# The store in SBUF, and the places that loads write into, moved to multiples of 256 bytes

## The chip, the cores and the metric

The kernel runs on one core of a Trainium2 chip. The core has five engines: TensorE (PE in the profile, with its weight loads as PEld), VectorE (DVE), ScalarE (ACT), GpSimd (POOL) and SyncE (SP), and it moves data with 16 DMA engines. Its on-chip memory SBUF has 128 partitions. The metric is the device time of one execution in microseconds (us): 740.67 us before the change, the median of three runs that lay between 740.43 and 740.8 us.

## The reference

Two layers of attention, each followed by a gated MLP, run one after the other on one token for a batch of 4, with the same weights both times. All data are float32.

```python
def _A_ref(x, k_cache, v_cache, wq, wo):           # x: 4 x 1 x 640
    q = (x @ wq)                                   # 640 x 4096: 32 heads of 128
    k, v = k_cache[:, :, -1024:], v_cache[:, :, -1024:]   # 4 x 32 x 1024 x 128 each
    p = softmax(q . k * 128 ** -0.5)
    return (p . v) @ wo                            # 4096 x 640
def _B_ref(x, W_gate, W_up, W_down):               # 640 x 1728, 640 x 1728, 1728 x 640
    gate, up = x @ W_gate, x @ W_up
    return (gate * (gate > 0) * up) @ W_down

x = x + _A_ref(layernorm(x), ...)
x = x + _B_ref(layernorm(x), ...)
x = x + _A_ref(layernorm(x), ...)
x = x + _B_ref(layernorm(x), ...)
```

The keys and values of the last 1024 positions, together 134 MB, are read once per layer, and so are the weights, except for what is kept on chip between the layers.

## The kernel before

The host lays all inputs that have to be loaded out as three wide arrays of 128 rows, one row to a partition. `heads` holds the query weights (q), keys (k), values (v) and output weights (o) of 27 heads in the order in which they are used, 255,744 floats to a row. `kept` holds the same for the last 5 heads, 47,360 floats to a row. `mlp` holds the weights of the MLP, 25,920 floats to a row. `heads` and `mlp` are loaded in both layers. `kept` is loaded once and stays in SBUF until the second layer's attention has used it.

Nearly all of SBUF is one tile, `store`, of `STORE` floats in each partition. The function `load` (L156) treats it as a ring: it takes the next piece of the list `todo`, finds the place `at` where it goes, cuts the piece where it would run over the end of the store or of a quarter of it (`QUARTERS`, for large pieces), and stops when a float of that place is still in use (`live`). Otherwise it issues one DMA on SyncE's queue (L185), which copies a range of columns of all 128 rows. `kept` has places of its own, at its own offsets, and where the ring starts anew is set by a few numbers: `FIRST` for the first layer's first pieces, `FIRST_MLP` for the first piece of the first layer's `mlp`, `FRONT` for what lies behind the kept heads. Each time a matmul's operand has been used, `done` frees its floats and calls `load` again. All this is done while the program is built. In the program there are 107 loads on one queue, each with the waits that its place needs. The first 1024 columns go to a tile of their own, `first_q` (L160).

A load copies one contiguous run of bytes into each partition, so a load of 13,312 columns is 128 rows of 53,248 bytes. The trace has one packet for each row, eight to a DMA engine, and one packet of 4 bytes per load and DMA engine. 64 of the 107 loads have rows of 8 KB and more, 30 of them rows of 52 to 55 KB (about 13,300 columns). The other 43 have shorter rows, down to 256 columns. They stand mainly in and around the first layer's MLP, where the ring has little room, because `kept` fills most of the store.

TensorE computes queries (L316, L321), scores (L345), transposes of the probabilities (L358), values (L373) and output projections (L403) group by group of up to four heads, and the MLP by L457, L492 and L501. It reads every operand straight out of the store. VectorE and ScalarE do the softmax and small copies.

Where the tiles lie follows from their sizes, in the order in which the pools allot them. The small tiles end at byte 9,440 of each partition, which is 36 x 256 + 224. So `store` begins 224 bytes behind a multiple of 256. Column c of the store has the address 9,440 + 4c. The ring mostly starts at column 0 or at multiples of 64 columns, so that nearly all loads begin 224 bytes behind a multiple of 256. The exceptions: the first four loads into the store, which start from `FIRST`, begin at 160; one load of the first `mlp` piece, at `FIRST_MLP`, begins at 128; `first_q` and one load of the second layer (rows of 53,376 bytes, at column 40,416) begin at 96. In HBM all rows begin on multiples of 256 bytes, except for that last load and one of 1,920-byte rows, which begin 128 behind.

Of the kernel before, what the change touches and what calls it, by code (L numbers as in the profile page):

```python
# [7 lines left out]
F32 = mybir.dt.float32  # L8
# [5 lines left out]
P = 128  # L14
# [43 lines left out]


HELD = 1024  # L60
STORE = 54944 - HELD
QUARTERS = [STORE // 4, STORE // 2, STORE // 4 * 3, STORE]
FRONT = KEPT * 2 * (D + KV)
FIRST, FIRST_MLP = 10928, 53160


def size_of(what, i):
# [23 lines left out]
def decode_kernel(ctx: ExitStack, tc: tile.TileContext, x, source, sel, out):  # L91
# [7 lines left out]
    ps_y = ctx.enter_context(tc.tile_pool(name="ps_y", bufs=1, space=bass.MemoryType.PSUM))  # L99
    ps_m = ctx.enter_context(tc.tile_pool(name="ps_m", bufs=2, space=bass.MemoryType.PSUM))  # L100
    big = ctx.enter_context(tc.tile_pool(name="big", bufs=1))
    store = big.tile([P, STORE], F32, name="store")
    first_q = big.tile([P, HELD], F32, name="first_q")
    ctx.enter_context(tc.manual_schedule())
# [45 lines left out]

    live = [False] * STORE
    at, spare = FIRST, True
# [3 lines left out]
    def load(part=False):  # L156
# [4 lines left out]
        while todo:  # L161
# [4 lines left out]

            ends = QUARTERS if end - lo > 16384 else [STORE]
            room = min(e - to for e in ends if e - to >= 2048 or e == STORE)
            hi = max(c for c in cuts if c <= min(end, lo + room))
# [413 lines left out]
```

## Time and profile before

| what | value |
|---|---|
| median of 3 runs | 740.67 us (740.43 to 740.8) |
| span of the profiled execution, first to last instruction | 738.5 us |
| the runs' median less that span | 2.2 us |
| PE busy | 453.3 us (61%) |
| DVE busy | 75.1 us (10%) |
| ACT busy | 47.1 us (6%) |
| packets of SyncE's load queue | 15,552, 312.24 MB |

The trace gives the span of the profiled execution; the only times of whole executions are those of the runs. The profile lists DMA queues with their packets, megabytes, and the time that their packets took as a share of what 16 DMA engines have in the stretch looked at. Such a row can be asked for any window of the span. It counts packets that begin in the window, and their whole time, so that a share can be a little over or under 100% in a short window; the share times 16 times the window's length, divided by the number of packets, is the mean time of one packet. SyncE's load queue is q1. The rows q8 and q14 are loads of instructions, and q10 is ScalarE's queue.

### The profile page before, as it was taken

The page shows a single profiled execution, that of the slowest core. Times are in us where ns is not written, and L with a number is a line of the kernel's source. Part 1 is how long each engine was busy: PE and PEld are TensorE (multiplying, and loading weights), DVE is VectorE, ACT ScalarE, POOL GpSimd, SP SyncE. Part 2 cuts the span into 40 slices and gives each one's busy share as a digit, 9 for nine tenths or more (in the row PEclk, how much of TensorE's full clock was granted, in tenths as well). Part 3 has the DMA queues.
Part 4 walks back from the last instruction along what each step waited for, and adds up shares of the span by engine and source line. Part 5 has one row for each costly group of instructions (what it writes and reads, how often), then busy time and mean ns, then how long its engine had stood idle before and what let it go on. Part 6 is the DMA issues. An engine that isn't in the chain of part 4 may idle for free.

```text
span 738.5 us, 8243 instructions
## 1 busy us (share of the span) xinstructions
PE 453.3 (61%) x3749; PEld 143.2 (19%) x3749; DVE 75.1 (10%) x279; ACT 47.1 (6%) x88; POOL 0.2 (0%) x4
## 2 busy tenths in 40 slices
PE   1657366556567636726689898445756545656685
PEld 0111111011122201202333232101211111122242
DVE  1011000010001001101101211001010100001010
ACT  1100000000000000000101110000000000000110
POOL 0000000000000000000000000000000000000000
PEclk9889787867689867969999999867778977668899
DMA  9999999999999999999999999999999999999996
GB/s 393 448 409 439 441 425 428 447 417 431 441 431 424 426 446 411 445 418 420 410 397 394 427 430 427 443 427 446 425 431 423 447 426 425 438 434 427 422 423 281
DMA packets 15738, 312.85 MB, mean 424 GB/s; under 512 B 1748, under 2 KB 2260, under 8 KB 7512
## 3 DMA queue, kind: packets, MB, share of 16 engines
q1 hardware_dynamic: 15552, 312.24, 99.0%
q8 instruction: 29, 0.48, 0.3%
q10 hardware_dynamic: 152, 0.09, 0.0%
q14 instruction: 5, 0.04, 0.0%
HBM read 312.24 MB, written 0.08 MB: 423 GB/s over the span
## 4 chain that ended last, share of the span: by engine, by line
DMA 52%; PE 32%; another core or an unknown queue 14%; issue 1%; DVE 1%; ACT 0%; SPq 0%; DVEq 0%; ACTq 0%
DMA store<-in_heads 30%; PE ps L345 13%; DMA store<-in_mlp 12%; PE po L373 10%; DMA store<-in_kept 10%; PE qp L316 2%; PE pp L358 1%; PE y L403 1%; PE qp L321 1%; PE gu L457 1%; PE qt L333 1%; PE ot L393 0%; PE po L258 0%; PE so L384 0%
## 5 line engine op out<-in xcount | busy, mean ns | idle before, releaser
L345 PE MATMUL ps<-store,qT 128*4 128x512 f32 x1024 | 161.3, 700 | 106.2 <-DMA store<-in_heads 101.1
L373 PE MATMUL po<-store,pT 128*16 128x512 f32 x1024 | 155.9, 720 | 108.0 <-DMA store<-in_heads 97.4
L373 PEld LDWEIGHTS po<-store,pT 128*16 128x16 f32 x1024 | 34.7, 110 | 214.1 <-issue 131.0
L345 PEld LDWEIGHTS ps<-store,qT 128*4 128x4 f32 x1024 | 29.3, 93 | 220.1 <-DMA store<-in_heads 116.1
L349 DVE TENSOR_REDUCE nm<-ps 128x1 f32<-128x1024 f32 x18 | 22.0, 1225 | 243.4 <-PE ps L345 243.4
L353 ACT ACTIVATE probs<-ps,nm 128x1024 f32<-128x1024 f32 x18 | 20.0, 1113 | 353.3 <-DVE nm L349 345.6
L316 PE MATMUL qp<-store,xT 128*32 128x512 f32 (+2 forms) x136 | 23.6, 623 | 24.6 <-DMA store<-in_heads 24.5
L403 PE MATMUL y<-store,oT 128*4 128x160 f32 x512 | 26.0, 332 | 8.8 <-DMA store<-in_heads 7.6
L369 DVE COPY pT<-pp 128x16 f32<-128x16 f32 x128 | 17.1, 168 | 135.6 <-PE po L373 135.6
L457 PE MATMUL gu<-store,xT 128*32 128x256 f32 (+1 forms) x300 | 23.9, 379 | 9.1 <-DMA store<-in_mlp 8.6
L380 ACT COPY gates<-po 128x512 f32<-128x512 f32 x16 | 9.4, 586 | 244.3 <-PE po L373 244.3
L358 PE MATMUL pp<-sel_sb,probs 128*128 128x128 f32 x144 | 20.5, 289 | 0.0
L358 PEld LDWEIGHTS pp<-sel_sb,probs 128*128 128x128 f32 x144 | 18.1, 151 | 0.0
L321 PE MATMUL qp<-store,xT 128*32 128x512 f32 (+4 forms) x48 | 17.5, 512 | 0.0
L326 DVE TENSOR_SCALAR gates<-qp,rstd 128x512 f32<-128x512 f32 (+2 forms) x18 | 12.4, 690 | 49.9 <-PE qp L321 44.5
L386 DVE RECIPROCAL r<-so 128x16 f32<-128x16 f32 x18 | 4.6, 257 | 122.6 <-PE so L384 122.6
L403 PEld LDWEIGHTS y<-store,oT 128*4 128x4 f32 x512 | 13.3, 93 | 19.4 <-DMA store<-in_heads 8.2
L457 PEld LDWEIGHTS gu<-store,xT 128*32 128x32 f32 x300 | 11.0, 115 | 18.1 <-DMA store<-in_mlp 7.4
L492 PE MATMUL y<-store,hT 128*4 128x160 f32 x208 | 11.3, 329 | 3.4 <-DMA store<-in_mlp 3.2
L333 PE MATMUL qt<-sel_sb,gates 128*128 128x128 f32 x64 | 12.3, 316 | 0.0
L393 PE MATMUL ot<-sel_sb,gates 128*128 128x128 f32 x72 | 11.4, 279 | 1.2 <-DVE gates L377 1.2
L333 PEld LDWEIGHTS qt<-sel_sb,gates 128*128 128x128 f32 x64 | 7.6, 155 | 18.6 <-issue 17.3
(62 smaller groups left out, 108.5 us busy)
## 6 DMA issues: line engine op xcount, KB each, us to landing
store<-in_heads SPq DMA_DIRECT2D x18, 6656.0 KB, 54.2
store<-in_heads SPq DMA_DIRECT2D x7, 6912.0 KB, 52.2
store<-in_heads SPq DMA_DIRECT2D x2, 6592.0 KB, 54.6
store<-in_heads SPq DMA_DIRECT2D x2, 5376.0 KB, 65.5
store<-in_mlp SPq DMA_DIRECT2D x16, 640.0 KB, 6.9
store<-in_kept SPq DMA_DIRECT2D x4, 2048.0 KB, 40.4
store<-in_heads SPq DMA_DIRECT2D x3, 2560.0 KB, 20.9
store<-in_heads SPq DMA_DIRECT2D x1, 6896.0 KB, 46.1
```

Source lines behind the costliest of these rows:

```text
L316: nc.tensor.matmul(qp[g][32 * c:32 * c + 32, :], xT[:, B * c:B * c + 32], part(layer, "q", g, c * n, n), start=True, stop=c > 0 and not sp ...
L321: nc.tensor.matmul(qp[g][32 * a:32 * a + 32, a * m:a * m + m], xT[:, B * c:B * c + 32], part(layer, "q", g, c * n + a * m, m), start=False ...
L326: nc.vector.tensor_scalar(gates[:, :len(HEADS[g]) * P], qp.pop(g), rstd, SCALE, op0=ALU.mult, op1=ALU.mult)
L333: nc.tensor.transpose(qt[:, i], gates[:, i * P:(i + 1) * P], ident)
L345: nc.tensor.matmul(ps[32 * b:32 * b + SIDE, j, :], qT[:, at:at + SIDE], part(layer, "k", h, lo, 512), start=i == 0, stop=i == n - 1, tile_ ...
L349: nc.vector.tensor_reduce(nm[g], ps.rearrange("p j n -> p (j n)"), axis=AX.X, op=ALU.max, negate=True)
L353: nc.scalar.activation(probs, ps.rearrange("p j n -> p (j n)"), AF.Exp, bias=nm.pop(g), accum_out=sums[g])
L358: nc.tensor.transpose(pps[g][c // 4][:, c % 4, :], probs[:, c * P:(c + 1) * P], ident)
L369: nc.vector.tensor_copy(to[:, 4 * j:4 * j + 4], pp[j][:, :, i:P:32])
L373: nc.tensor.matmul(po[32 * a:32 * a + SIDE * B, :], t[:, at:at + SIDE * B], part(layer, "v", h, c * 512, 512), start=i == 0 and c < 4, sto ...
L403: nc.tensor.matmul(y[32 * a:32 * a + B], o[:, i], part(layer, "o", h, a * QUARTER, QUARTER), start=False, stop=last and h == HEADS[g][-1], ...
L457: nc.tensor.matmul(gus[j][32 * g:32 * g + 32, :2 * n], xT[:, B * c:B * c + 32], get(layer, "mlp", lo, 2 * n), start=c == 0, stop=c == KC - ...
```

## The change

The constants become multiples of 64 floats, and a tile of 8 floats (32 bytes) that nothing uses is allotted ahead of the store:

```diff
 HELD = 1024
-STORE = 54944 - HELD
+STORE = 53888
 QUARTERS = [STORE // 4, STORE // 2, STORE // 4 * 3, STORE]
 FRONT = KEPT * 2 * (D + KV)
-FIRST, FIRST_MLP = 10928, 53160
+FIRST, FIRST_MLP = 10944, 53248
...
     big = ctx.enter_context(tc.tile_pool(name="big", bufs=1))
+    big.tile([P, 8], F32, name="pad")
     store = big.tile([P, STORE], F32, name="store")
```

The store now begins at byte 9,472 = 37 x 256 and has 53,888 floats instead of 53,920. `first_q` follows it at 225,024 = 879 x 256. All loads but one begin on a multiple of 256 bytes in SBUF. The exception is the load of 53,376-byte rows, which begins 128 behind one (its rows in HBM begin 128 behind one too). The lines of the kernel below the new tile have numbers higher by one.

The instructions of TensorE, VectorE, ScalarE and GpSimd are the same, in the same order. On SyncE's queue two pairs of neighbouring loads are cut elsewhere, because the end of the store has moved by 32 floats. The first pair is the last `heads` piece of the first layer, where it runs over the end of the store (the names are the tile written and the array read, then partitions x columns). On SP, before:

```order
L185 DMA store<-in_heads 128x2560
L185 DMA store<-in_heads 128x13728
L185 DMA store<-in_heads 128x480
L185 DMA store<-in_kept 128x8192
L185 DMA store<-in_kept 128x4096 x4
```

and now:

```order
L186 DMA store<-in_heads 128x2560
L186 DMA store<-in_heads 128x13568
L186 DMA store<-in_heads 128x640
L186 DMA store<-in_kept 128x8192
L186 DMA store<-in_kept 128x4096 x4
```

160 columns have moved from the first load to the second.

The second pair is in the first layer's MLP, where the ring comes to the end of the store for the first time. On SP, before:

```order
L185 DMA store<-in_mlp 128x512
L185 DMA store<-in_mlp 128x768
L185 DMA store<-in_mlp 128x1280 x3
L185 DMA store<-in_mlp 128x512
L185 DMA store<-in_mlp 128x768 x2
L185 DMA store<-in_mlp 128x512
```

and now:

```order
L186 DMA store<-in_mlp 128x512
L186 DMA store<-in_mlp 128x768
L186 DMA store<-in_mlp 128x1280 x3
L186 DMA store<-in_mlp 128x768
L186 DMA store<-in_mlp 128x512
L186 DMA store<-in_mlp 128x768
L186 DMA store<-in_mlp 128x512
```

The load of 512 columns and the first of 768 behind the three of 1280 have changed places, and so 256 columns have moved from the second to the first. In both kernels the second of the pair waits for TensorE to have used the load at `FIRST_MLP`.

## The prediction

> **What bounds the kernel now.** I read the page's DMA part first, then the windows by stage, then the chain.
>
> ```profile
> span 738.5 us, 8243 instructions
> ...
> DMA  9999999999999999999999999999999999999996
> ...
> DMA packets 15738, 312.85 MB, mean 424 GB/s; under 512 B 1748, under 2 KB 2260, under 8 KB 7512
> ...
> q1 hardware_dynamic: 15552, 312.24, 99.0%
> q8 instruction: 29, 0.48, 0.3%
> q10 hardware_dynamic: 152, 0.09, 0.0%
> q14 instruction: 5, 0.04, 0.0%
> ...
> DMA 52%; PE 32%; another core or an unknown queue 14%; issue 1%; DVE 1%; ACT 0%; SPq 0%; DVEq 0%; ACTq 0%
> ```
>
> The 16 DMA engines are busy in every slice but the last, and the load queue q1 alone takes 99.0% of their time. The windows by stage (first layer's attention, its MLP, two parts of the second attention, second MLP; busy time of each engine, granted clock, DMA share, GB/s) say the same:
>
> ```profile
> 2.00:361.00 359.00, 202.32 (x1507) 57.39 (x1511) 33.80 (x124) 22.05 (x36) 0.00 (x0) 0.81 1.00 430
> 361.00:402.00 41.00, 34.40 (x432) 14.27 (x428) 4.55 (x19) 4.28 (x14) 0.00 (x0) 1.00 1.01 397
> 402.00:464.00 62.00, 55.51 (x472) 17.73 (x464) 12.44 (x39) 6.95 (x12) 0.00 (x0) 0.94 1.01 425
> 464.00:712.00 248.00, 143.48 (x1072) 43.53 (x1071) 20.86 (x83) 12.11 (x22) 0.00 (x0) 0.79 1.00 432
> 712.00:738.50 26.50, 17.57 (x283) 10.27 (x283) 2.43 (x10) 1.67 (x5) 0.00 (x0) 0.87 0.78 324
> ```
>
> The DMA share is 1.00 up to 712 us, while PE, the next engine, is busy for about three fifths of the time. The chain ends on a load as well, followed by one set of matmuls and a copy:
>
> ```profile
> 712.18 22.84 DMA store<-in_mlp
> ...
> 735.07 0.50 PE y L492 x8
> ...
> 735.59 0.32 DVE probs L523
> ```
>
> So a nanosecond saved on a packet should reach the end, times the packets that one DMA engine has in sequence. There are 107 loads of 8 rows for each engine, 856 rows (with the output's store, 108 x (128 + 16) gives the row's 15,552). Of all packets 15,738 - 7,512 = 8,226 have 8 KB or more; less the 34 of q8 and q14 these are 8,192, or 512 long rows to an engine, and 344 are short.
>
> **What a row costs now.** A row's time is its bytes at some rate, and something besides. Two rows of the DMA view part them, one of mostly long rows (window 70 to 240 us) and one of shorter ones (418 to 462 us):
>
> ```profile
> q1 hardware_dynamic: 1536, 73.30, 99.9%
> ...
> q1 hardware_dynamic: 1100, 18.77, 100.3%
> ```
>
> The first is 0.999 x 16 x 170 = 2717.3 us of packet time, the second 1.003 x 16 x 44 = 706.1 us. Scaled to the first one's megabytes (x 3.905) the second has 4,296 packets and 2757.4 us: 2,760 more packets take 40.1 us more, 14.5 ns each. What is left of the first is 27.2 bytes per ns and DMA engine. At most 14.5 x 856 = 12.4 us of the kernel, then, is beside the bytes.
>
> Next, windows that hold rows of one length and one start alone, in this order: 14.7 to 21.4 us (55,296 bytes, starting 160 behind a multiple of 256), 39.6 to 53.7 (53,248 at 160), 71.5 to 84.5 (53,248 at 224), 103 to 117.3 (55,296 at 224), 310.1 to 322.3 (54,912 at 224), 563 to 576.3 (55,168 at 224) and 579.3 to 589.6 (53,376 at 96):
>
> ```profile
> q1 hardware_dynamic: 50, 2.76, 95.2%
> ...
> q1 hardware_dynamic: 112, 5.96, 97.8%
> ...
> q1 hardware_dynamic: 110, 5.86, 104.2%
> ...
> q1 hardware_dynamic: 112, 6.19, 100.2%
> ...
> q1 hardware_dynamic: 96, 5.27, 100.1%
> ...
> q1 hardware_dynamic: 100, 5.52, 96.1%
> ...
> q1 hardware_dynamic: 82, 4.38, 98.1%
> ```
>
> Share x 16 x length / packets gives means of 2041.1, 1970.0, 1970.3, 2046.9, 2035.4, 2045.0 and 1971.6 ns. Less the bytes at 27.2 per ns, the extra is 8.2, 12.3, 12.7, 14.0, 16.6, 16.8 and 9.2 ns. The first window, before the DMA engines have been held up, stands apart. The other six go by one count: how many 256-byte blocks of SBUF a row touches, each at 256 / 27.2 = 9.41 ns whether it is filled or not. These are 209, 209, 217, 216, 217 and 209 blocks. The measured means lie 2.9, 3.2, 4.5, 2.5, 2.6 and 4.5 ns above, a spread of 2.0 instead of 7.6. A row of whole blocks that starts at 160 or 224 touches one block more than it fills; the 54,912- and 55,168-byte rows waste one and a half, and the 53,376-byte row only half of one. I take this as the reason why rows cost 13 ns beside their bytes and not 8.
>
> **The change part by part.** *Starts on multiples of 256 bytes.* A row of whole blocks then wastes none. What remains is the cost of a packet that nothing holds up. The lower end is the block count alone: the 9.4 ns of one block are saved on each of 856 rows, 8.1 us. The other end is the 9.2 ns of the 53,376-byte row, the best in the steady stretches: 4.0 ns saved. Between them I take the 8.2 ns of the first window, since it has the same odd start and still runs below its block count (217 x 9.41 = 2042.4 ns), so it shows another limit, of the packet itself.
>
> Long rows: the mean of 12.7 and 14.0, the two common lengths, is 13.3, and 13.3 - 8.2 is 5.1 ns. Of 512 rows 16 are in the first two loads, of which I take it that they cost 8.2 already; 496 x 5.1 = 2.5 us. Short rows: two windows of 5,120-byte rows, 368.3 to 368.8 and 382.6 to 383.1 us, read
>
> ```profile
> q1 hardware_dynamic: 42, 0.22, 105.0%
> ...
> q1 hardware_dynamic: 40, 0.20, 99.0%
> ```
>
> or 200.0 and 198.0 ns against 188.2 for the bytes: 11.8 and 9.8, mean 10.8, so 2.6 ns x 344 = 0.9 us. With 9.2 in place of 8.2 it is 4.1 x 496 + 1.6 x 344 = 2.6 us.
>
> Here a rule stands against a row. The Trainium skill, "DMA: Bandwidth & Descriptors", section "How a descriptor splits into AXI transactions", says that a first transaction begins at the 256-byte boundary below the start, and that the unused bytes still cost beats of 32 bytes. By it a start at 224 costs 7 beats, one at 160 costs 5, and alignment saves an estimated 7.0 us. The trace does not agree on the step between them, 12.7 against 12.3 ns where the rule has 2.4 ns, and no run here shows a start at 0.
>
> *The part that does not reach the end.* In the first layer's MLP the chain runs for a while on TensorE, from
>
> ```profile
> 381.24 0.62 PE gu L457 x2
> ...
> 390.58 0.40 PE y L492 x6
> ...
> 390.99 6.05 DMA store<-in_mlp
> ```
>
> 9.7 us, in which earlier data are worth nothing. About seven loads land in it; 7 x 8 x 2.6 ns is 0.15 us. I take off 0.3 us, since later loads there wait for places that TensorE frees.
>
> *The two pairs that are cut elsewhere.* Bytes and count stay. The first pair lies under a queue that is 43 us deep (its 480-column piece, 240 KB, from issue to landing):
>
> ```profile
> store<-in_heads SPq DMA_DIRECT2D x1, 240.0 KB, 42.8
> ```
>
> so where it is cut costs nothing while that queue is there, and without it the 160 columns that change sides, 8 x 640 bytes / 27.2 = 0.2 us. In the second pair the first load grows by 256 columns and lands 8 x 1,024 / 27.2 = 0.3 us later; the second ends where it did. At 0 to 0.3 us I take 0, since TensorE needs the second right after. The unused tile issues nothing. That TensorE's operands start elsewhere I price at nothing: PE is hidden under the DMA share of 1.00 above, and no row shows a price by start.
>
> Sum: 2.5 + 0.9 - 0.3 = 3.1 us off the span of 738.5, or 735.4. What lies around the span, 2.2 us up to the median of 740.67, is not touched. That gives **737.6 us**, 0.4% less. With 9.2 ns a row it is 738.4, and the rounding of the shares, 1 ns a row or 0.9 us, widens the two to 736.7 and 739.3.
>
> **The rivals.** *The whole block is saved.* If the 8.2 ns of the first window are themselves due to the odd start, all 856 rows gain up to 9.4 ns, and the time is 740.7 - 8.1 = 732.6 us. For it speaks that the block count fits six windows to 2 ns; against it, that the first window does not follow it. The rule named above would give nearly this, an estimated 733.7 us.
>
> *No change.* The hold-up may be on the HBM side, or in handing out packets, and only look like a count of blocks, since just three kinds of waste occur. That 160 and 224 cost the same speaks for it. Then it stays at 740.7, give or take 0.5. Against it: the 53,376-byte rows are longer than the 53,248-byte ones by 4.7 ns worth of bytes and take only 1.3 ns more.
>
> *Slower: the engines in step.* The uneven hold-ups keep the 16 DMA engines apart. When they start together, on the first load (2.4 to 3.2 us, 4,096-byte rows),
>
> ```profile
> q1 hardware_dynamic: 58, 0.24, 88.4%
> ```
>
> a row takes 195.1 ns for 150.6 ns of bytes, 36 ns over the 8.2. If freed engines fell into step and a fifth of the rows paid that, it were 0.2 x 856 x 36 = 6.2 us, less the 3.1 gained: 743.8 us. It decides from about 10% of the rows on (3.1 / (856 x 0.036)). Against it: ten microseconds after that start the first window above shows only 8.2.
>
> **How the numbers follow.** My forecast gets 0.52: the block count is well borne out, the floor is a choice. The whole block gets 0.18, no change 0.20, slower 0.10. The range 732.5 to 741.0 us takes in my case, no change and the whole-block case at its full price, and leaves out a little over one in ten. A difference under 0.2%, 1.5 us, can hardly be told from none. Faster than that are my case but for its weak end (0.50) and the whole block: 0.68. The same: 0.22. Slower: 0.10.
>
> **What would show it.** In the changed kernel a window of 53,248-byte rows should read 1965.8 ns a row instead of 1970.3 (1961 if the whole block goes, 1970 if nothing does), with hardly any step between the first microseconds and later. Rows of 5,120 bytes should read 196.4. The load at 128 behind a multiple (53,376-byte rows) should stay near 1971.6. The page's mean should rise from 424 to about 426 GB/s, with q1 still at 99%. The forecast fails if rows do get shorter but the queue then stands empty, with SP waiting for TensorE, or if the packets cost the same.

## The result

The changed kernel takes 736.33 us (median of 5 runs, 736.1 to 738.37) against 740.8 us for the kernel before in the same comparison (740.43 to 741.24). The ratio is 0.9941, with a 95% interval of 0.993 to 0.9952: 4.4 us less, between 3.6 and 5.2. The span of the profiled execution fell from 738.5 to 734.5 us, by 4.1 before rounding.

The page of the changed kernel, the rows that answer to those shown of the kernel before:

```profile
span 734.5 us, 8243 instructions
...
DMA packets 15738, 312.85 MB, mean 426 GB/s; under 512 B 1748, under 2 KB 2132, under 8 KB 7512
...
q1 hardware_dynamic: 15552, 312.24, 99.1%
q8 instruction: 29, 0.48, 0.2%
...
DMA 54%; PE 30%; another core or an unknown queue 14%; issue 1%; DVE 1%; ACT 0%; SPq 0%; DVEq 0%; ACTq 0%
```

The same packets and bytes, on a queue that is as full as before (99.1%, 99.0% before). Nothing else took over as the bound. The chain ends as it did, on the same load and the same matmuls, 4.1 us earlier:

```profile
708.31 22.62 DMA store<-in_mlp
...
730.98 0.50 PE y L493 x8
```

The windows by stage, those of the first attention and the first MLP (the last figure is GB/s, 430 and 397 before):

```profile
2.00:361.00 359.00, 202.66 (x1519) 57.96 (x1519) 33.81 (x124) 22.06 (x36) 0.00 (x0) 0.81 1.00 432
361.00:402.00 41.00, 35.49 (x443) 15.19 (x443) 5.76 (x22) 5.24 (x15) 0.00 (x0) 1.00 1.02 407
```

The row times are read as in the prediction, from windows of the DMA view that hold rows of one length alone: 14.6 to 21.1 us (55,296 bytes), 39.9 to 53.9 and 71.3 to 85.3 (53,248), 102.8 to 116.3 (55,296), 309.4 to 322 (54,272), 559.7 to 572.9 (55,168), 576 to 586.1 (53,376, starting 128 behind a multiple of 256) and 366.9 to 367.6 (5,120):

```profile
q1 hardware_dynamic: 56, 3.10, 109.9%
...
q1 hardware_dynamic: 112, 5.96, 98.3%
...
q1 hardware_dynamic: 112, 5.96, 98.3%
...
q1 hardware_dynamic: 109, 6.03, 103.0%
...
q1 hardware_dynamic: 101, 5.48, 100.4%
...
q1 hardware_dynamic: 100, 5.52, 96.4%
...
q1 hardware_dynamic: 81, 4.32, 98.8%
...
q1 hardware_dynamic: 56, 0.29, 98.0%
```

These are 2041.0, 1966.0, 1966.0, 2041.1, 2004.0, 2036.0, 1971.1 and 196.0 ns a row, or 8.1, 8.4, 8.4, 8.2, 8.7, 7.8, 8.7 and 7.8 ns over the bytes at 27.2 per ns. Before, the extra was 9 to 17 ns in the windows from 39.6 us on. In these windows it now stays where it stood in the first microseconds, for every length. (The rounding of a share to 0.1% is worth about 1 ns a row in the windows of long rows.)

The windows are a choice, so the packets of the whole of both traces were added up too. The long rows (8 KB and more) average 13.2 ns over their bytes before and 8.3 now, the short ones 11.2 and 8.4. Left out are the rows that took over 100 ns extra, 28 long ones in either trace and 82 short ones before, 76 now; 26 of the 28 in each trace run while an instruction load of q8 or q14 is under way, against one in eleven of the other long rows.

### The profile page after: what moved, and what is told of

Its sections match the earlier page's. It is cut to its first block, busy times and chain, and to the rows that moved or that the text cites. A ratio compares the mean times of both kernels' runs of the same rounds, so it can differ in the third digit from the quotient of the medians.

```text
span 734.5 us, 8243 instructions
## 1 busy us (share of the span) xinstructions
PE 452.5 (62%) x3749; PEld 142.7 (19%) x3749; DVE 75.0 (10%) x279; ACT 47.1 (6%) x88; POOL 0.2 (0%) x4
## 3 DMA queue, kind: packets, MB, share of 16 engines
q1 hardware_dynamic: 15552, 312.24, 99.1%
## 4 chain that ended last, share of the span: by engine, by line
DMA 54%; PE 30%; another core or an unknown queue 14%; issue 1%; DVE 1%; ACT 0%; SPq 0%; DVEq 0%; ACTq 0%
DMA store<-in_heads 32%; PE ps L346 12%; DMA store<-in_mlp 12%; DMA store<-in_kept 10%; PE po L374 9%; PE y L404 1%; PE qp L317 1%; PE pp L359 1%; PE qp L322 1%; PE gu L458 1%; PE qt L334 1%; PE ot L394 0%; PE po L259 0%; PE y L493 0%
## 5 line engine op out<-in xcount | busy, mean ns | idle before, releaser
L374 PE MATMUL po<-store,pT 128*16 128x512 f32 x1024 | 155.2, 718 | 105.4 <-DMA store<-in_heads 95.4
L458 PE MATMUL gu<-store,xT 128*32 128x256 f32 (+1 forms) x300 | 26.3, 414 | 8.3 <-DMA store<-in_mlp 7.9
L370 DVE COPY pT<-pp 128x16 f32<-128x16 f32 x128 | 17.1, 168 | 135.3 <-PE po L374 135.3
L327 DVE TENSOR_SCALAR gates<-qp,rstd 128x512 f32<-128x512 f32 (+2 forms) x18 | 12.4, 691 | 48.4 <-PE qp L322 44.4
L359 PEld LDWEIGHTS pp<-sel_sb,probs 128*128 128x128 f32 x144 | 17.1, 146 | 0.0
L404 PEld LDWEIGHTS y<-store,oT 128*4 128x4 f32 x512 | 13.3, 93 | 19.5 <-DMA store<-in_heads 8.0
L334 PE MATMUL qt<-sel_sb,gates 128*128 128x128 f32 x64 | 12.3, 316 | 0.0
L334 PEld LDWEIGHTS qt<-sel_sb,gates 128*128 128x128 f32 x64 | 7.6, 155 | 18.8 <-issue 17.5
## 6 DMA issues: line engine op xcount, KB each, us to landing
store<-in_kept SPq DMA_DIRECT2D x4, 2048.0 KB, 39.9
```

The lines of the kernel that those rows point to most:

```text
L327: nc.vector.tensor_scalar(gates[:, :len(HEADS[g]) * P], qp.pop(g), rstd, SCALE, op0=ALU.mult, op1=ALU.mult)
L334: nc.tensor.transpose(qt[:, i], gates[:, i * P:(i + 1) * P], ident)
L359: nc.tensor.transpose(pps[g][c // 4][:, c % 4, :], probs[:, c * P:(c + 1) * P], ident)
L370: nc.vector.tensor_copy(to[:, 4 * j:4 * j + 4], pp[j][:, :, i:P:32])
L374: nc.tensor.matmul(po[32 * a:32 * a + SIDE * B, :], t[:, at:at + SIDE * B], part(layer, "v", h, c * 512, 512), start=i == 0 and c < 4, sto ...
L404: nc.tensor.matmul(y[32 * a:32 * a + B], o[:, i], part(layer, "o", h, a * QUARTER, QUARTER), start=False, stop=last and h == HEADS[g][-1], ...
```

## Experiments

### The two halves of the change

The tile alone, in the kernel before. 100 of the 107 loads then start on a multiple of 256, and the first four of the store at 192 behind one:

```diff
     big = ctx.enter_context(tc.tile_pool(name="big", bufs=1))
+    big.tile([P, 8], F32, name="pad")
     store = big.tile([P, STORE], F32, name="store")
```

> The kernel before with the 32-byte tile alone: the store starts on a multiple of 256 bytes, 100 of 107 loads start on one, the first four of the store at 192 behind one, and the constants are the old ones. Block count (a row costs the 256-byte blocks that it touches): as the changed kernel, 736.3 to 736.9 us. If the new constants matter for another reason (other cuts, another place of the ring): 739 us or more.

The constants alone, in the changed kernel:

```diff
-    big.tile([P, 8], F32, name="pad")
```

> The changed kernel without the 32-byte tile: the same cuts and order of loads, but 106 of 107 loads start 224 behind a multiple of 256. Block count: as before, 740.2 to 741.0 us, with 1970 ns for a row of 53,248 bytes. If the cuts make the gain: about 736.5 us.

The tile alone took 736.37 us, ratio 0.9938 (0.9925 to 0.9952); the constants alone took 740.63 us, ratio 0.9999 (0.9991 to 1.0008). So the 32 bytes are the whole gain, and the new cuts are worth nothing that can be measured. The trace of the tile alone has both kinds of start within one execution. Rows of 53,248 bytes from 39.8 to 53.8 us, at 192, and from 71.5 to 85.5 us, at 0:

```profile
q1 hardware_dynamic: 112, 5.96, 98.5%
...
q1 hardware_dynamic: 112, 5.96, 98.3%
```

1970.0 ns and 1966.0 ns. With the constants alone, at 224 (71.9 to 84.6 us), it is 1970.5:

```profile
q1 hardware_dynamic: 109, 5.80, 105.7%
```

### Which starts count

In the kernel before all starts but one were 32 behind a multiple of 64, and none was equal to the start in HBM. So a multiple of 64 might be enough, or equal starts. Three variants of the changed kernel:

```diff
-    big.tile([P, 8], F32, name="pad")
+    big.tile([P, 40], F32, name="pad")
```

> The changed kernel with a tile of 160 bytes in place of 32, so that all loads but one start 128 behind a multiple of 256. Block count: one block wasted per row as before, 740.2 to 741.0 us, 1970 ns for a row of 53,248 bytes. If a multiple of 64 bytes is enough (all starts before were 32 behind one, but for one load): as the changed kernel, 736.3 us, 1966 ns. If the cost grows with the bytes ahead of the start: in between, about 738.5 us.

The same, and the rows in HBM 128 bytes further on:

```diff
+LEAD = 32
...
-            nc.sync.dma_start(out=store[:, to:to + hi - lo], in_=source[row][:, lo:hi])
+            nc.sync.dma_start(out=store[:, to:to + hi - lo], in_=source[row][:, LEAD + lo:LEAD + hi])
...
-        "heads": laid["heads"],
+        "heads": np.pad(laid["heads"], ((0, 0), (LEAD, LEAD))),
```

and so for `kept`, `mlp` and `first_q`.

> As the start at 128, and the three arrays in HBM have 32 floats of zeros ahead of each row (and 32 behind), so that the loads start 128 behind a multiple of 256 in HBM too. Block count in SBUF: as before, 740.2 to 741.0 us. If what counts is that source and destination have the same start (in the changed kernel they do, in the kernel before none did): as the changed kernel, 736.3 us.

And the rows in HBM moved on with the small tile left at 32 bytes:

> The changed kernel, its starts in SBUF on multiples of 256, with the rows in HBM 128 bytes further on (32 floats of zeros ahead of each row and 32 behind). Block count in SBUF: the start in HBM does not matter, 736.3 us, 1966 ns for a row of 53,248 bytes. If source and destination have to have the same start, or the source has to start on a multiple of 256: 739 to 741 us, 1970 ns.

| start in SBUF, start in HBM | us | ratio (95% interval) |
|---|---|---|
| 128, 0 | 739.83 | 0.9984 (0.9975 to 0.9993) |
| 128, 128 | 739.66 | 0.9984 (0.9975 to 0.9993) |
| 0, 128 | 736.39 | 0.9943 (0.9929 to 0.9957) |

The start in HBM does not matter, and 128 is nearly as dear as 224: the two starts at 128 took 0.4 and 0.5 us less than the lower end of what the block count gave, 740.2 us. The rows of 53,248 bytes of the three, in that order (71.7 to 84.9, 71.6 to 84.9 and 71.5 to 84.3 us), read 1969.9, 1968.9 and 1966.1 ns:

```profile
q1 hardware_dynamic: 110, 5.86, 102.6%
...
q1 hardware_dynamic: 111, 5.91, 102.7%
...
q1 hardware_dynamic: 110, 5.86, 105.6%
```

The first of the three, the start at 128, gains 0.9 us that the block count does not have. It lies in the rows: the packets of q1 in its trace, added up, take 0.8 us less to a DMA engine than with the constants alone, which start at 224. Why 128 is a little cheaper than 224 is open.

### Loads alone

To see the disputed cost by itself, two kernels issue nothing but loads on SyncE's queue, ten of each kind after one another, and write zeros as their output. Each ran once (constants are put in as numbers here):

```python
for i, (dst, src, over) in enumerate(CASES):
    n = 64 * (96 + i) + over // 4
    for _ in range(10):
        to = at % 7 * 7680 + dst // 4
        lo = at % 30 * 7680 + src // 4
        nc.sync.dma_start(out=store[:, to:to + n], in_=source[:, lo:lo + n])
        at += 1
```

> Loads alone, nothing is computed and the output is zeros: 9 x 10 loads of 128 rows into seven places of a store, rows of 96 to 104 whole blocks of 256 bytes (24,576 to 26,624 bytes, one block more in each group of ten), starting in SBUF at 224, 0, 32, 64, 128, 160, 16, 4 and 256 behind a multiple of 512 plus 256. Extra time of a row over its bytes at 27.2 per ns. Block count: 8.3 ns at 0 and 256, 12 to 13.5 ns at all others. Bytes ahead of the start: growing from 32 to 224. Multiples of 64 bytes: 8.3 also at 64 and 128. If a start off a multiple of 32 bytes costs something of its own: 16 and 4 dearer than 32.

The first, in the order of its starts, each in a window late in its group (from 32.4, 105.4, 179, 253.9, 329.5, 405.8, 483, 569.5 and 656 us, 6 to 7.1 us long):

```profile
q1 hardware_dynamic: 112, 2.75, 106.9%
...
q1 hardware_dynamic: 110, 2.73, 103.8%
...
q1 hardware_dynamic: 112, 2.81, 99.2%
...
q1 hardware_dynamic: 112, 2.84, 97.2%
...
q1 hardware_dynamic: 112, 2.87, 94.0%
...
q1 hardware_dynamic: 112, 2.90, 97.7%
...
q1 hardware_dynamic: 112, 2.92, 100.3%
...
q1 hardware_dynamic: 108, 2.85, 105.4%
...
q1 hardware_dynamic: 108, 2.88, 104.1%
```

| start | 224 | 0 | 32 | 64 | 128 | 160 | 16 | 4 | 256 |
|---|---|---|---|---|---|---|---|---|---|
| window, us | 6.0 | 6.1 | 6.6 | 6.8 | 7.1 | 6.9 | 6.8 | 6.3 | 6.4 |
| row, ns | 916.3 | 921.0 | 935.3 | 944.2 | 953.4 | 963.0 | 974.3 | 983.7 | 987.0 |
| over its bytes, ns | 12.8 | 8.1 | 12.9 | 12.4 | 12.2 | 12.4 | 14.3 | 14.3 | 8.2 |

There is a step between a multiple of 256 and all other starts. A share's rounding is worth 0.5 ns in these rows. Among multiples of 32 bytes, which other start it is makes less than 1 ns. Starts at 16 and 4 cost 1.4 to 2.1 ns more than those, which the block count does not have. Neither the bytes ahead of the start nor a multiple of 64 count. No TensorE reads the store here, so the cost is between the DMA engines and the memories.

The hold-up can also take time to set in. The group at 32 follows the one at 0, and the rows of its first load (149.5 to 156 us) still read 931.4 ns, 9.0 over the bytes. Those of its third load (165.2 to 170.9 us) still read 931.0, 8.6 over the bytes, before they come to 12.9:

```profile
q1 hardware_dynamic: 112, 2.81, 100.3%
...
q1 hardware_dynamic: 96, 2.41, 98.0%
```

So some three loads, 22 us, pass first. The kernel before shows the like at its start: its rows, off the multiples of 256 from the first load on, read 8.2 ns in the window from 14.7 to 21.4 us and 12.3 in the one from 39.6 us.

> Loads alone as before, output zeros, rows of 96 to 105 blocks and a remainder (start in SBUF, start in HBM, bytes over whole blocks): (0,0,32), (0,0,128), (0,0,224), (32,0,-32), (128,0,128), (224,0,32), (224,0,128), (0,128,0), (128,128,0), (0,32,0). Block count, as the larger of 8.3 ns and 3.4 ns and the unfilled bytes at 27.2 per ns: 11.6, 8.3, 8.3, 8.3, 8.3, 11.6, 17.5, 8.3, 12.8, 8.3 ns. If only the start counts: 8.3 wherever the first number is 0, 12 to 13 elsewhere. If equal starts count: 8.3 for (128,128,0), 12 to 13 for (0,128,0) and (0,32,0).

The second kernel, in the order of its cases (from 54.2, 105.6, 180, 254.8, 330.2, 414.3, 492, 562.8, 656.9 and 720.3 us; 6.3, 6.7, 6.7, 6.7, 6.8, 6.8, 6.9, 6.0, 6.7 and 6.7 us long):

```profile
q1 hardware_dynamic: 112, 2.76, 102.0%
...
q1 hardware_dynamic: 112, 2.80, 96.9%
...
q1 hardware_dynamic: 112, 2.83, 98.1%
...
q1 hardware_dynamic: 112, 2.83, 98.1%
...
q1 hardware_dynamic: 112, 2.88, 98.2%
...
q1 hardware_dynamic: 113, 2.93, 100.3%
...
q1 hardware_dynamic: 112, 2.94, 99.6%
...
q1 hardware_dynamic: 101, 2.66, 102.9%
...
q1 hardware_dynamic: 110, 2.93, 101.7%
...
q1 hardware_dynamic: 110, 2.96, 102.2%
```

| start in SBUF, in HBM, bytes over whole blocks | unfilled bytes of the blocks touched | expected, ns | measured over the bytes, ns |
|---|---|---|---|
| 0, 0, 32 | 224 | 11.6 | 13.3 |
| 0, 0, 128 | 128 | 8.3 | 9.8 |
| 0, 0, 224 | 32 | 8.3 | 8.4 |
| 32, 0, -32 | 32 | 8.3 | 8.4 |
| 128, 0, 128 | 128 | 8.3 | 8.1 |
| 224, 0, 32 | 224 | 11.6 | 14.0 |
| 224, 0, 128 | 384 | 17.5 | 17.1 |
| 0, 128, 0 | 0 | 8.3 | 8.6 |
| 128, 128, 0 | 256 | 12.8 | 12.3 |
| 0, 32, 0 | 0 | 8.3 | 7.8 |

The first and the fourth row decide it. A row that starts on a multiple of 256 but ends 32 bytes into a block pays 13.3 ns, and one that starts 32 bytes late but ends on a multiple pays 8.4. The sixth row rules out that the end alone counts: it ends on a multiple and pays 14.0 ns. Nor is it the end in HBM, which lies 32 bytes into a block in the first row too, since in the last row it does so as well, and 7.8 ns are paid. So it is the blocks touched in SBUF that count, at either end, and not the start.

The sizes are met to within 2.4 ns only. With 224 unfilled bytes a row costs 1.7 and 2.4 ns more than the formula has, and more than the rows of whole blocks with 256 unfilled bytes (12.3 here, 12.2 to 12.9 above). 128 unfilled bytes cost more at the end of a row than at its start. What makes these differences is open.

Nor does the hold-up always set in late. The group of the sixth row follows three that show no hold-up, and the rows of its first load (376 to 382 us) read 964.0 ns, 12.2 over the bytes, at once:

```profile
q1 hardware_dynamic: 96, 2.49, 96.4%
```

### What the short rows are worth

The landings of loads in the two traces differ by 1.3 us at 360 us and by 2.4 us at 405 us, so the first layer's MLP seemed to give 1.1 us of the gain, more than its packets. To measure it, the ring of that stage alone was moved, once off the multiples of 256 in the changed kernel, and once onto them with the constants alone:

```diff
-                at = FRONT if layer == 0 and row == "mlp" else KEPT * D if layer == 1 and spare else 0
+                at = FRONT + 8 if layer == 0 and row == "mlp" else KEPT * D if layer == 1 and spare else 0
...
-    jumps = {(0, "heads", turn[0]): 2 * KEPT * D, (0, "mlp", 0): FIRST_MLP, (1, "heads", HELD): FRONT}
+    jumps = {(0, "heads", turn[0]): 2 * KEPT * D, (0, "mlp", 0): FIRST_MLP, (1, "heads", HELD): FRONT + 8}
```

> The changed kernel with the ring of the first layer's MLP moved on by 8 floats: the 29 loads in and behind that stage (232 short rows to a DMA engine) start 32 behind a multiple of 256, all others on one. The second pair of loads is cut as in the kernel before. If the rows alone count, 2.8 ns x 232 = 0.65 us more than the changed kernel. If the short rows are worth more than their packets, as the landings of the two traces suggest (about 1.1 us between 360 and 405 us): 1.0 to 1.3 us more.

> The other way round: the constants alone, without the tile, and the same 8 floats, so that only those 29 loads start on a multiple of 256 and all others 224 behind one. If the rows alone count, 0.65 us less than before, 740.1 us. If short rows are worth more: 1.0 to 1.3 us less, 739.6 us.

> The changed kernel once more, beside the last two on the same chip: 736.3 us, with a mean of 8.3 ns over the bytes for long rows.

On the same chip the changed kernel took 736.42 us, ratio 0.994 (0.9926 to 0.9955); its rows of 53,248 bytes (71.5 to 85.5 us) again read 8.4 ns over their bytes. With the stage moved off it took 737.23 us, 0.9955 (0.9938 to 0.9972). With the stage alone moved on it took 739.87 us against 740.71 us before, 0.999 (0.9979 to 1.0001). The 29 loads are worth 0.8 us either way: between what was expected of their rows alone (0.65) and the 1.1 us of the landings. The windows from 361 to 402 us of the three, in the order of their expectations:

```profile
361.00:402.00 41.00, 35.01 (x439) 14.92 (x431) 5.37 (x22) 5.23 (x15) 0.00 (x0) 1.00 1.02 401
...
361.00:402.00 41.00, 35.12 (x441) 14.79 (x442) 4.85 (x20) 4.89 (x14) 0.00 (x0) 1.00 1.01 402
...
361.00:402.00 41.00, 35.84 (x443) 15.22 (x443) 5.77 (x22) 5.24 (x15) 0.00 (x0) 1.00 1.02 410
```

410 GB/s with the stage aligned in the changed kernel, 401 without; with the stage alone moved on it is 402, against 397 before. The changed kernel itself read 407 in the result, so two executions of one kernel differ by 3 GB/s. The differences of 0.8 us lie within the intervals of the single comparisons, but the runs hardly overlap: 11 of the 12 with the stage alone moved on are below all 17 of the kernel before, and all 6 with the stage moved off are above 5 of the 6 of the changed kernel. The time of q1's packets, added up from the traces, differs by 0.8 us between the changed kernel and the stage moved off, and by 0.7 between the constants alone and the stage alone moved on. So the packets' own time is about all of it. The stage moved off also has the second pair of loads cut as before, and shows nothing beside the rows.

## Why the prediction was right

*The bound.* The queue was full and stayed full, and a shorter row reached the end. This held.

*What a row costs.* The step rested on counting 256-byte blocks from seven windows of the trace. The loads alone bear it out with starts and ends that the kernel never had, though not every size, and the variants exclude its rivals: starts equal to those in HBM, multiples of 64, and the cuts. The packet's own 8.2 ns, taken from the first window, was the right floor, and the loads alone show why that window could stand apart: the hold-up can take some 22 us to set in. Forecast were 1965.8 ns for rows of 53,248 bytes, 196.4 for 5,120 and 1971.6 for 53,376; measured were 1966.0, 196.0 and 1971.1, closer than the rounding of the shares can vouch for. Over all rows but the few very long ones, 4.9 ns went from a long row and 2.8 from a short one, where the forecast had 5.1 and 2.6.

*The sum.* 3.1 us were forecast and 4.4 measured. So 736.33 us lies inside the range, but below the 736.7 to 739.3 us that the forecast gave its own case. The two row terms were right; three smaller things were not, all the same way.

- The two row terms, 2.5 + 0.9 us, are borne out. The packets of q1, added up one by one from the two traces, took 731.5 us to a DMA engine before and 728.0 now, 3.5 us less.
- The 0.3 us taken off for the first layer's MLP, on the ground that the chain runs on TensorE there, were not lost: aligning that stage's 29 loads is worth 0.8 us at the end.
- The time in which no packet of q1 is on record, what is left of the span, went from 7.1 to 6.4 us, about 0.6 us that my sum did not have. That the gaps between packets shrink with the hold-ups would explain it, but this was not tested.
- What lies around the span was put at 2.2 us. In every run of the record whose span is known, before and after alike, a run takes 1.7 to 1.9 us more than its span. The span of 738.5 us belongs to a run faster than the median, and so the forecast started 0.4 us too high.

*Whole block saved.* Ruled out: an aligned row still takes 8 ns over its bytes, so that aligning it saves about 5 ns of the 9.4 ns of a block.

*No change.* Ruled out by the step from 8.1 to 12.9 ns between starts at 0 and 32 in one execution, without any other work.

*The engines in step.* Ruled out: in all eight windows, from 14 us to 587 us, rows read 7.8 to 8.7 ns over their bytes, with no trace of the first load's 36 ns, and the rows with over 100 ns extra are no more than before.

*The rule weighed there.* The Trainium skill, "DMA: Bandwidth & Descriptors", section "How a descriptor splits into AXI transactions", has the bytes between a 256-byte boundary and the start cost beats of 32 bytes, which from a start at 32 to one at 224 would be 6 beats, an estimated 7 ns. It has a leftover at the row's end cost only its own beats. Its words are about reads, and a load reads HBM and writes SBUF. On the SBUF side neither holds: starts at 32 and 224 read 12.9 and 12.8 ns, no growth at all, and 32 bytes over at the end read 13.3 ns. On the HBM side, starts at 32 and 128 added nothing to a row, 7.8 and 8.6 ns.

The tile of 32 bytes alone is as fast as the whole change. No variant was faster.

## What to carry to other kernels

Where one DMA queue is full from end to end, look at what a row costs beside its bytes, in windows that hold rows of one length alone: here it was 12 to 17 ns on long rows, and 5 of them went with one tile of 32 bytes. Let rows begin and end on multiples of 256 bytes in SBUF; a row with 32 bytes over at its end paid as much as one with an odd start, and where the row starts in HBM did not matter. Read such costs from stretches well behind the first microseconds, since the hold-up took up to some 22 us to set in here. Read them first in the windows of the profile, which gave the row times here to within their rounding, about 1 ns, before anything was tried.

## What was not expected

An aligned row with 32 bytes over whole blocks is dearer (13.3 ns) than a misaligned one without (12.2 to 12.9 ns at starts of 32 to 224). In the first kernel of loads alone, rows off the multiples still ran at 8.6 to 9.0 ns for three whole loads before they came to 12.9, as if something between the two sides had first to fill; in the second, one group was held up at once. What decides it, no run here shows.
